# A gated recurrence with a highway layer on one core: the last product written in place, in four pieces, and a new order of all operations

## The chip, the core and the metric

The kernel runs on one core of a Trainium2 chip. Five engines work side by side, each through its own queue of instructions in order: TensorE (PE) multiplies matrices and transposes, VectorE (DVE) and ScalarE (ACT) work on tiles elementwise, GpSimd (POOL) does so more slowly and not out of PSUM, and SyncE (SP) here only issues the DMAs between the memory of the device (HBM) and the on-chip memory (SBUF). TensorE writes to PSUM. The metric is the time of one execution in device microseconds, the median of several runs.

## The reference

25344 tokens (4 sequences of 6336) of 256 channels. A recurrence along each sequence, and a highway layer on its result:

```python
    sig = 1.0 / (1.0 + np.exp(-f_logit))
    f = lower_bound[None, None, :] + (1.0 - lower_bound[None, None, :]) * sig
    i = 1.0 - f
    ...
    for t in range(S):
        h = f[:, t] * h + i[:, t] * x[:, t]
        y[:, t] = h
    ...
    H = np.maximum(x @ w_h, 0.0)
    T = 1.0 / (1.0 + np.exp(-(x @ w_t + b_t)))
    return (T * H + (1.0 - T) * x).astype(np.float32)
```

In the last three lines x stands for y of the recurrence. The result is x + T * (max(x w_h, 0) - x), and max(x w_h, 0) - x is max(x w_h - x, -x).

## The kernel before

The tokens are cut into 28 units in order: two of 256 tokens, one of 512, 23 of 1024, one of 512 and one of 256. A unit holds nb = 2, 4 or 8 blocks of 128 tokens. Per unit, with a letter for each operation (the number behind it is the unit, the one behind the point the half of the channels h or m, the block group or the piece):

- l and x load f_logit and x (SP's queue), up to 1 MB each; u = sigmoid(-l) on ScalarE.
- b (L277 to L283) is bv = u * x, in pieces of two blocks (128x512 per piece), on GpSimd, or on VectorE where the token ends in v.
- i and p transpose u and bv on TensorE into PSUM, so that channels lie on partitions and tokens along the free axis. f = 1 - (1 - lower_bound) u on ScalarE (VectorE with v).
- s (L321) is the recurrence itself, a scan along the tokens on VectorE out of f and the transposed bv. It needs the carry of the unit before, so all the s of one half stand in one chain.
- g and z (`ffn`, L329) are the two matrix products on y; t (L348) is the sigmoid of z on ScalarE; d (L352) is max(y * ncc, g) on VectorE, out of y and the PSUM of g. The factor 1 - lower_bound that the recurrence leaves out is folded into the weights and into ncc.
- E and e (L357 to L365) are e = d * t. The list `units` holds a cut for each unit: up to it, E computes in pieces of 512 on GpSimd; from it to the end (2 * tokens), one e does the rest on VectorE. There are 59 E and 16 e.
- o (L370) adds diag * y and e on TensorE, which also transposes back, in groups of four blocks; c copies it out of PSUM on ScalarE (one on VectorE); w writes it out over SP's queue.

Every tile has a tag made of its name and a slot number, `name:slot` in the list; a tile with a tag that was used before takes over that buffer once all that read the old one has run. Before, u, bv, y (4), d, t and e have three slots, f and the outputs o four, l and x six. In PSUM there are two slots of one bank (uT, bT) and three of two banks (z, g, op).

The order is written by hand as one long list of tokens, `order`: each engine gets its instructions in the order of the list (`pin` is `tc.keep_in_program_order`), and nothing reorders them. Waits between engines follow from the data and the slots. One wait is added by hand, `shared` (L203 to L209): the last VectorE instruction that is marked as sharing is held, and the next GpSimd product in the list waits for its end:

```python
        if not gpsimd:
            held[:] = [ins]
        elif held:
            tc.add_manual_dep(ins.ins, held.pop().ins.name, mybir.DependencyInfo(
                mybir.DependencyClass.Sync, mybir.DependencyReason.DATA), reason="shared port")
```

There is no such wait of VectorE for GpSimd.

Of the kernel before, what the change touches and what calls it, by code (L numbers as in the profile page):

```python
# [19 lines left out]
def kernel(  # L20
# [10 lines left out]
    nc = tc.nc  # L31
# [10 lines left out]
    units = [  # L42
        (0, 128, 2, 0, 'y', 4, 512),
        (0, 128, 2, 256, 'y', 4, 512),
        (0, 128, 4, 512, 'y', 4, 1024),
        (0, 128, 8, 1024, 'y', 4, 512),
        (0, 128, 8, 2048, 'y', 4, 512),
        (0, 128, 8, 3072, 'y', 4, 1792),
        (0, 128, 8, 4096, 'y', 4, 2048),
        (0, 128, 8, 5120, 'y', 4, 0),  # L50
        (0, 128, 8, 6144, 'y', 4, 0),
        (0, 128, 8, 7168, 'y', 4, 2048),
        (0, 128, 8, 8192, 'y', 4, 0),
        (0, 128, 8, 9216, 'y', 4, 1280),
        (0, 128, 8, 10240, 'y', 4, 2048),
        (0, 128, 8, 11264, 'y', 4, 2048),
        (0, 128, 8, 12288, 'y', 4, 2048),
        (0, 128, 8, 13312, 'y', 4, 512),
        (0, 128, 8, 14336, 'y', 4, 512),
        (0, 128, 8, 15360, 'y', 4, 512),  # L60
        (0, 128, 8, 16384, 'y', 4, 512),
        (0, 128, 8, 17408, 'y', 4, 2048),
        (0, 128, 8, 18432, 'y', 4, 256),
        (0, 128, 8, 19456, 'y', 4, 2048),
        (0, 128, 8, 20480, 'y', 4, 2048),
        (0, 128, 8, 21504, 'y', 4, 2048),
        (0, 128, 8, 22528, 'y', 4, 1024),
        (0, 128, 8, 23552, 'y', 4, 0),
        (0, 128, 4, 24576, 'y', 4, 768),
        (0, 128, 2, 25088, 'y', 4, 256),  # L70
    ]
# [21 lines left out]
b13.2 c9.1:2 i15.1:1 p12.0:0 g11.1:0 e10:2 f15.1:1 i13.0:1 w9.1 z11.1:2 t11.0:2 s12.0 o9.0:1 p13.0:0 b14.2:2 f13.0:2
t11.1 l16:4 i14.1:1 o10.1:2 b14.3 c9.0:3 f14.1:0 E11.0:0 z12.1:1 p13.1:1 b14.0 x16:4 c10.1:1 d11.1 b14.1 s13.0:0
o10.0:0 e11 w9.0 g12.0:2 t12.1:0 i15.0:0 b15.0:0 b15.1 c10.0:0 z12.0:1 s13.1 p14.1:1 f15.0:2 z13.0:0 t12.0 i14.0:0
E11.2 g12.1:1 E11.1 d12.0:0 l17:5 b15.3 g13.0:2 u16:2 s14.1:2 d12.1 t13.0:1 p14.0:1 f14.0:3 o11.1:0 o11.0:1 E12.0:1
c11.1:2 i16.0:0 b16.1:1 d13.0:1 g13.1:2 b16.3 w10.1 E12.1 w10.0 s14.0 z13.1:0 b15.2 E12.2 c11.0:3 x17:5 p15.0:1 b16.2
b16.0 E12.3 f16.0:0 l18:0 p15.1:0 d13.1 w11.0 u17:0 z14.0:1 w11.1 o12.0:2 l20:1 s15.0:3 t13.1 i16.1:1 c12.0:1 E13.3:2
w12.0 f16.1:3 s15.1 g14.0:0 x18:0 E13.0 o12.1:2 E13.1 d14.0:2 p16.1:0 t14.0:2 E13.2 z14.1:1 b17.3:2 c12.1:0 g14.1:0
u18:1 p16.0:1 s16.1:1 t14.1 z15.1:2 i17.0:0 d14.1 t15.1:0 b17.0 o13.1:0 f17.0:2 g15.0:1 b17.2 l19:2 g15.1:2 c13.1:3  # L100
s16.0 w12.1 w13.1 d15.0:0 b17.1 i17.1:1 x19:1 u20:2 o13.0:0 z15.0:1 p17.0:0 E14.2:0 f17.1v:1 d15.1 E14.0 c13.0:2
i18.0:1 z16.1:2 t15.0 g16.0:0 b18.0:0 f18.0:3 t16.1:1 E14.3 E14.1 s17.0:0 i20.0:1 l21:3 b18.1 p17.1:0 d16.0:1 b18.2
# [5 lines left out]
p20.1:0 e17 w15.1 x22:4 s20.0:1 o17.1:0 l23:5 z19.0:2 w16.1 t19.1:1 w16.0 l24:0 s20.1 i21.0:1 c17.1:3 b21.2 t19.0
g19.1:1 g19.0:0 b21.1 E18.0:1 i22.0:0 b21.3 e18 x23:5 o17.0:2 d19.1:1 l25:1 f21.0:0 f22.0:3 b22.3:1 c17.0:2 p21.0:1
u23:2 b22.1 p21.1:0 d19.0 x24:0 z20.0:1 w17.0 s21.0:0 o18.0:0 b22.2 b22.0 o18.1:2 i23.0:1 c18.0:1 g20.1:0 t20.0:2  # L110
s21.1 d20.1:2 g20.0:1 E19.2:2 p22.1:0 c18.1:0 w18.0 z21.1:2 u24:1 E19.0 E19.1 f23.0:0 w17.1 d20.0 z20.1:0 i24.1:1
E19.3 b23.3:2 s22.1:2 g21.1:1 t21.1:0 f24.1:1 t20.1 u25:0 b23.1 g21.0:2 i23.1:1 w18.1 p22.0:0 d21.1:0 l26:2 o19.0:0
d21.0 z21.0:2 s22.0 b23.0 f23.1:2 b23.2 E21.2:0 o19.1:1 t21.0 b24.3:0 p23.1:1 i25.0:0 z22.0:2 c19.1:2 x25:1 c19.0:1
l27:3 e20:1 g22.1:1 t22.0:1 w19.1 E21.0 b24.0 b24.1 s23.1:3 E20.0 b24.2 o20.1:0 p23.0:1 z22.1:2 f25.0:3 d22.1:1
i24.0:0 g22.0:1 E21.3 c20.1:3 s23.0 o20.0:0 t22.1 f24.0:2 E21.1 b25.1:1 c20.0:0 b25.2 p24.0:1 z23.0:2 d22.0 z23.1:1
w19.0 b25.0 s24.0:1 b25.3 g23.0:0 t23.0:2 w20.1 E22.1:2 t23.1 p24.1:0 u26:2 d23.0:2 o21.0:2 i25.1:1 g23.1:1 u27:1
x26:2 f25.1:0 E22.3 E22.0 x27:3 s24.1 o21.1:0 p25.0:1 c21.0:2 w20.0 i27.0:0 E22.2 d23.1 w21.0 f27.0:2 g24.0:2 i26.0:0
# [316 lines left out]
```

## Time and profile before

| | |
|---|---|
| runs, us | 212.19, 211.85, 211.55 (median 211.85) |
| span of the profiled execution, first to last instruction | 210.1 us |
| what lies around the span (median less span) | 1.75 us |
| granted TensorE clock, mean | 0.996 |
| moved by DMA | 78.69 MB, 374 GB/s over the span |

The profile gives the span of the profiled execution and no other time of it. Groups of the profile by line (busy is the time in which at least one of the group ran; instructions of one engine overlap a little at their ends):

| line, engine, result | count | busy us | mean ns |
|---|---|---|---|
| L282 POOL bv of 512 | 96 | 110.2 | 1178 |
| L359 POOL e of 512 | 54 | 61.8 | 1167 |
| L359 POOL e of 256 | 5 | 3.4 | 670 |
| L359 DVE e of 256, 768, 1024 | 3, 1, 1 | 0.8, 0.6, 0.7 | 280, 630, 684 |
| L359 DVE e of 1536, 1792, 2048 | 6, 1, 4 | 5.7, 1.1, 4.8 | 954, 1068, 1215 |
| L325 DVE scan of 1024 | 40 | 93.4 | 2340 |
| L354 DVE d of 1024 | 46 | 57.4 | 1263 |
| L282 DVE bv of 512 | 3 | 2.1 | 721 |
| L299 ACT f of 1024 | 45 | 52.8 | 1181 |
| L350 ACT t of 1024 | 46 | 53.1 | 1177 |
| L388 ACT o of 1024 | 48 | 51.1 | 1077 |

The DMA engines are at their full share up to about 175 us, and at half of it or less from 180 to 200 us. A digit of the page's slices is the busy share of a fortieth of the span, in tenths; a row of the timeline is the start and the duration in us, the engine, the line, the operation, its result and operands with shapes, the number of instructions merged into the row, and in brackets the idle time before it with what ended it.

### The profile page before, as it was taken

Reading aid. Unit: us, or ns where it says so; the run is one execution under the profiler, and the core shown is the slowest. Engines: PE = TensorE matmul, PEld = TensorE weight load, DVE = VectorE, ACT = ScalarE, POOL = GpSimd, SP = SyncE. Lnnn points to the kernel's source line nnn. Section 1 sums busy time; section 2 is a strip of 40 time slices with the busy share of each in tenths; the row PEclk is TensorE's granted clock in tenths of the full one; section 3 lists DMA queues with packets and bytes.
Section 4 is the critical chain, followed back from the end, with each engine's and each line's share of the span. In section 5 each row is a group of like instructions: output and inputs, shape, how many; then the busy total and the mean of one; then the engine's idle time right before and its main releaser. Section 6 shows DMA issues by size and latency. Waiting matters only on the chain.

```text
span 210.1 us, 4667 instructions
## 1 busy us (share of the span) xinstructions
PE 192.2 (91%) x1819; PEld 132.4 (63%) x1819; DVE 193.0 (92%) x154; ACT 194.5 (93%) x190; POOL 174.0 (83%) x166
## 2 busy tenths in 40 slices
PE   7967798899989989999999999999999899999981
PEld 2444555576655766767576667657775676776760
DVE  0689999999999999999999999999999999999950
ACT  4678999999999999999999999999999999997882
POOL 3068989789999599978999999889879969999630
PEclk9999999999999999999999999999999999999998
DMA  6999999999999999999999999999999998463486
GB/s 223 392 426 421 410 418 424 420 415 420 410 428 413 420 420 403 331 406 387 387 427 416 409 416 423 418 417 396 333 428 416 416 413 332 188 271 132 172 328 254
DMA packets 15982, 78.69 MB, mean 374 GB/s; under 512 B 1748, under 2 KB 2264, under 8 KB 10072
## 3 DMA queue, kind: packets, MB, share of 16 engines
q1 hardware_dynamic: 15952, 78.39, 92.9%
q8 instruction: 14, 0.23, 0.5%
q14 instruction: 8, 0.07, 0.1%
q10 hardware_dynamic: 8, 0.00, 0.0%
HBM read 52.43 MB, written 25.95 MB: 373 GB/s over the span
## 4 chain that ended last, share of the span: by engine, by line
DVE 34%; PE 34%; DMA 12%; issue 8%; POOL 5%; ACT 3%; SPq 1%; POOLq 0%; DVEq 0%; ACTq 0%
DVE y L325 21%; DMA x<-in_x_dram 12%; DVE d L354 10%; PE op L379 5%; PE op L378 5%; PE g L337 4%; PE z L337 4%; PE bT L308 4%; POOL bv L282 4%; PE g L140 4%; PE uT L288 4%; PE z L140 3%; DVE e L359 3%; ACT t L350 2%; ACT o L388 1%
## 5 line engine op out<-in xcount | busy, mean ns | idle before, releaser
L282 POOL TENSOR_TENSOR bv<-u,x 128x512 bf16<-128x512 f16 x96 | 110.2, 1178 | 22.3 <-DVE w_sb L235 8.9
L325 DVE TENSOR_TENSOR_SCAN y<-f,y,bT 128x1024 bf16<-128x1024 f16 (+5 forms) x54 | 107.2, 1994 | 1.4 <-issue 0.4
L359 POOL TENSOR_TENSOR e<-d,t 128x512 bf16<-128x512 bf16 (+1 forms) x59 | 65.0, 1125 | 8.3 <-DVE e L359 5.0
L354 DVE SCALAR_TENSOR_TENSOR d<-y,ncc,g 128x1024 bf16<-128x1024 bf16 (+2 forms) x56 | 63.1, 1140 | 1.8 <-PE g L337 1.3
L350 ACT ACTIVATE t<-z,bt 128x1024 bf16<-128x1024 f32 (+2 forms) x56 | 58.4, 1066 | 2.7 <-PE z L140 1.5
L299 ACT ACTIVATE f<-uT,ncc 128x1024 f16<-128x1024 f16 (+2 forms) x54 | 57.8, 1079 | 2.0 <-ACT f L299 1.0
L388 ACT COPY o<-op 128x1024 f32<-128x1024 f32 (+1 forms) x50 | 52.3, 1058 | 1.9 <-PE op L379 1.0
L274 ACT ACTIVATE u<-l 128x2048 f16<-128x2048 f32 (+2 forms) x28 | 49.0, 1760 | 4.1 <-DMA l<-in_f_logit_dram 4.1
L378 PE MATMUL op<-diag,y 128*128 128x128 f16 x396 | 49.4, 219 | 0.8 <-ACT t L350 0.5
L379 PE MATMUL op<-ident_b,e 128*128 128x128 bf16 x396 | 49.4, 219 | 0.6 <-POOL e L359 0.6
L379 PEld LDWEIGHTS <-e 128*128 128x128 bf16 x396 | 44.0, 113 | 4.6 <-POOL e L359 1.1
L378 PEld LDWEIGHTS <-y 128*128 128x128 bf16 x396 | 44.2, 113 | 2.5
L337 PE MATMUL z<-y,w_sb 128*128 128x512 bf16 (+1 forms) x112 | 39.2, 367 | 2.0 <-DVE d L354 1.0
L337 PE MATMUL g<-y,w_sb 128*128 128x512 bf16 (+1 forms) x112 | 39.6, 367 | 0.5 <-DVE y L325 0.3
L308 PE MATMUL bT<-ident_f,bv 128*128 128x128 f32 x198 | 31.9, 278 | 4.1 <-DVE y L325 1.9
L288 PE MATMUL uT<-ident_h,u 128*128 128x128 f16 x396 | 31.1, 220 | 4.5 <-DVE y L325 3.3
L288 PEld LDWEIGHTS <-u 128*128 128x128 f16 x396 | 26.3, 98 | 13.9 <-issue 7.4
L140 PE MATMUL g<-y,w_sb 128*128 128x512 bf16 x92 | 34.9, 379 | 0.0
L140 PE MATMUL z<-y,w_sb 128*128 128x512 bf16 x92 | 34.8, 379 | 0.0
L337 PEld LDWEIGHTS <-w_sb 128*128 128x128 f16 x224 | 21.6, 98 | 16.2 <-issue 0.8
L308 PEld LDWEIGHTS bT<-ident_f,bv 128*128 128x128 f32 x198 | 22.3, 141 | 12.0 <-POOL bv L282 4.5
L140 PEld LDWEIGHTS <-w_sb 128*128 128x128 f16 x184 | 17.9, 98 | 18.2 <-issue 3.9
(35 smaller groups left out, 47.1 us busy)
## 6 DMA issues: line engine op xcount, KB each, us to landing
out_dram<-o SPq DMA_DIRECT2D x48, 512.0 KB, 6.1
l<-in_f_logit_dram SPq DMA_DIRECT2D x23, 1024.0 KB, 10.2
x<-in_x_dram SPq DMA_DIRECT2D x23, 1024.0 KB, 11.1
l<-in_f_logit_dram SPq DMA_DIRECT2D x2, 512.0 KB, 9.2
x<-in_x_dram SPq DMA_DIRECT2D x2, 512.0 KB, 6.0
l<-in_f_logit_dram SPq DMA_DIRECT2D x3, 256.0 KB, 6.1
x<-in_x_dram SPq DMA_DIRECT2D x3, 256.0 KB, 5.4
out_dram<-o SPq DMA_DIRECT2D x3, 256.0 KB, 5.4
```

The costliest lines, as they stand in the source:

```text
L140: return pe.add_instruction(mybir.InstMatmult(name=nc.get_next_instruction_name(), start_tensor_calc=start, stop_tensor_calc=stop, tile_si ...
L282: shared(pin(e.tensor_mul(st[n]["bv"][:, k].rearrange("p d j -> p j d"), st[n]["u"][:, q:q + 2], st[n]["x"][:, q:q + 2])), not eng)
L288: pin(nc.tensor.transpose(uT[:, j * P:(j + 1) * P], st[n]["u"][:, j, h * P:(h + 1) * P], ident_h))
L299: pin(nc.scalar.activation(to, of, AF.Identity, scale=ncc[:, h:h + 1], bias=1.0))
L308: pin(nc.tensor.transpose(words[:, k:k + g * (P - 1) + 1:g], pair, ident_f))
L325: pin(nc.vector.tensor_tensor_scan(y[:, c:e], st[n]["f", h][:, c:e], st[n]["bT", h][:, c:e], 0.0 if fresh else carry[h], op0=ALU.mult, op1 ...
L337: pin(nc.tensor.matmul(p[:, a:e], w, half(n, "y", ki)[:, a:e], start=ki == 0, stop=ki == NH - 1))
L350: pin(nc.scalar.activation(half(n, "t", m), st[n]["z", m][:, :tokens(n)], AF.Sigmoid, bias=bt[:, m:m + 1]))
L354: pin(nc.vector.scalar_tensor_tensor(half(n, "d", m), half(n, "y", m), ncc[:, m:m + 1], st[n]["g", m][:, :tokens(n)], op0=ALU.mult, op1=AL ...
L359: shared(pin(eng.tensor_mul(st[n]["e"][:, a:e], st[n]["d"][:, a:e], st[n]["t"][:, a:e])), eng is nc.gpsimd)
L378: pin(nc.tensor.matmul(o, half(n, "y", h)[:, cols], diag[:, h], start=True, stop=False))
L379: pin(nc.tensor.matmul(o, half(n, "e", h)[:, cols], ident_b, start=False, stop=True))
```

## The change

The cut per unit is gone. `do_e` computes one of two (256-token units: 256 wide; 512: 512 wide) or four pieces of 512 and writes it over d; the token says by a v at its end that VectorE does it, and else GpSimd. There is no tile e any more, and o reads d:

```diff
-    def times(n, eng, a, e, slot):
-        flat(n, "e", "e", slot)
-        shared(pin(eng.tensor_mul(st[n]["e"][:, a:e], st[n]["d"][:, a:e], st[n]["t"][:, a:e])), eng is nc.gpsimd)
-
-    def do_E(n, k, eng, slot):
-        times(n, nc.gpsimd, k * 512, min(units[n][6], k * 512 + 512), slot)
-
     def do_e(n, k, eng, slot):
-        times(n, nc.vector, units[n][6], NH * tokens(n), slot)
+        a, c = units[n][3][k:k + 2]
+        e = nc.vector if eng else nc.gpsimd
+        shared(pin(e.tensor_mul(st[n]["d"][:, a:c], st[n]["d"][:, a:c], st[n]["t"][:, a:c])), not eng)
...
-                pin(nc.tensor.matmul(o, half(n, "e", h)[:, cols], ident_b, start=False, stop=True))
+                pin(nc.tensor.matmul(o, half(n, "d", h)[:, cols], ident_b, start=False, stop=True))
```

The units are the same, written by a formula; b is written with the same pieces of two blocks:

```diff
+    parts = [2] * 2 + [4] + [8] * 23 + [4] + [2]
+    units, at = [], 0
+    for nb in parts:
+        units.append((nb, at, {2: (0, 1), 4: (0, 1, 2), 8: (0, 1, 2, 3, 4)}[nb], {2: (0, 256, 512), 4: (0, 512, 1024), 8: (0, 512, 1024, 1536, 2048)}[nb]))
+        at += nb * P
```

The list is a new one from the first token to the last. Its beginning and end before and after:

```diff
-pc:1 l0:0 u0:0 l3:1 wh cc dg i0.0:1 x0:0 i0.1:0 k*16 u3:1 wt WH b0.0v:0 l1:2 f0.0:0 f0.1:1 p0.1:0 i3.1:1 u1:2 s0.1:0
+l1:0 x0:0 x1:1 wt l0:1 u1:0 wh l2:2 l3:3 b1.0v:0 x2:2 x3:3 l4:0 pc:0 x4:4 i1.0:0 l7:4 cc i1.1:1 u0:0 b0.0:1 l5:5 dg
+f1.1:0 k*16 f1.0v:1 u2:1 i0.1:0 WH i0.0:1 f0.0:2 f0.1v:3 p0.0:0 WT p0.1:1 s0.0:0 s0.1 b2.0:1 i2.0:0 f2.0v:2 u3:0 b2.1
+g0.1:0 p1.0:1 z0.1:1 z0.0:2 s1.0:1 t0.1:0 p1.1:0 s1.1 i3.0:1 d0.1:0 t0.0 f3.0:0 i2.1:0 g1.0:1 b3.1:0 x5:1 f2.1v:1 b3.2
+z1.1:0 g1.1:2 t1.1:1 p2.1:0 i3.1:1 g0.0:0 b3.0 f3.1:3 d1.1:1 e1.1 z1.0:2 e0.1 b3.3v u4:1 d0.0 s2.1:2 p2.0:1 s2.0
...
-E26.1 w24.1 d27.0 z27.0:2 c25.1:1 w25.0 t27.0 E26.0 o26.0:1 w25.1 c26.0:3 e27:0 E27.0 o27.0:2 c27.0:0 w26.0 w27.0
+s27.0:0 w23.1 c24.0:1 s27.1 g26.0:1 t26.0 d26.0:0 g26.1:0 e25.2 c25.1:3 d26.1 w24.1 w23.0 e26.0v w24.0 z27.0:2 t27.1:0
+w25.1 o25.0:1 g27.0:0 e26.1v c25.0:0 o26.0:2 d27.0:1 z27.1:0 t27.1 g27.1:1 c26.0:1 w25.0 w26.0 d27.1 e27.1v e27.0v
+o27.0:0 c27.0:2 w27.0
```

What the two lists hold, counted:

| | before | after |
|---|---|---|
| bv on GpSimd, on VectorE | 96, 3 | 97, 2 |
| e on GpSimd: of 512, of 256 | 54, 5 | 61, 3 |
| e on VectorE | 16, of 256 to 2048 | 35 of 512, 3 of 256 |
| f on VectorE | one of 1024, one of 256 | two of 512, two of 256 |
| o copied by VectorE | one of 512 | one of 1024 |
| slots named: u, bv, d | 3, 3, 3 | 4, 3, 4 |
| slots named: l, x | 6, 6 | 6, 5 |

More of the change, by code (lines that the diff above doesn't have):

```diff
@@ L39 @@
     firsts = [b * S for b in range(B)]
[L42 to L71, printed above, removed]
@@ L93 @@
[L93 to L97, printed above, removed]
@@ L98 @@
[L98 to L102, printed above, removed]
@@ L108 @@
[L108 to L112, printed above, removed]
@@ L113 @@
[L113 to L117, printed above, removed]
@@ L118 @@
-c21.1:1 o22.1:1 s25.0:0 f26.0:1 E23.2:1 b26.0:2 z24.0:0 p25.1:0 d24.0:0 c22.1:3 b26.1 t24.0:0 E23.0 i26.1:1 z24.1:1
-f26.1:3 o22.0:0 g24.1:2 E23.1 w21.1 i27.1:1 s25.1 w22.1 t24.1 g25.0:1 c22.0:0 z25.0:0 b27.0:0 d24.1 d25.0:1 p26.0:0
-f27.1:0 E23.3 o23.0:2 p26.1:1 E24.0:0 z25.1:1 t25.0:1 g25.1:0 s26.0:2 c23.0:2 s26.1 z26.0:2 t25.1 d25.1 p27.1:1
-t26.0:2 o23.1:1 g26.1:2 e24 s27.1:3 o24.0:0 d26.1:2 c23.1:1 w22.0 z26.1:1 E24.1 c24.0:3 p27.0:1 w23.0 w23.1 t26.1
-e25:2 s27.0 w24.0 o24.1:2 c24.1:0 g26.0:0 o25.0:1 g27.1:2 c25.0:2 d26.0 o25.1:0 e26:1 d27.1:0 g27.0:2 z27.1:1 t27.1:0
@@ L123 @@
[L123 removed]
+    parts = [2] * 2 + [4] + [8] * 23 + [4] + [2]
[3 more added lines that the diff above has]
+        at += nb * P
+    assert at == B * S
+    order = """
+l1:0 x0:0 x1:1 wt l0:1 u1:0 wh l2:2 l3:3 b1.0v:0 x2:2 x3:3 l4:0 pc:0 x4:4 i1.0:0 l7:4 cc i1.1:1 u0:0 b0.0:1 l5:5 dg
@@ new lines @@
+e10.3 t11.0:0 b15.2:0 b15.0 x14:0 t11.1 o9.0:2 l18:2 b15.3 i14.1:0 e11.0 b15.1 b14.2:2 e11.1v b14.0 o9.1:0 f14.1:0
+p13.0:1 b14.1 e11.3v e11.2v s13.0:1 z12.1:1 c9.1:0 c9.0:2 i15.1:0 e10.1v g12.1:0 f15.1:2 z12.0:2 p13.1:1 d12.1:2 x17:1
+i15.0:0 s13.1 t12.1:0 o10.1:0 t12.0 f15.0:3 g12.0:1 b14.3 e12.2 g13.0:2 e12.3 i14.0:0 w9.1 c10.1:1 g13.1:0 u18:0 d12.0
+d13.0:3 l16:0 o10.0:1 p14.1:1 d13.1 f14.0:1 c10.0:3 s14.1:2 z13.0:2 b17.1:1 z13.1:0 p14.0:0 w9.0 s14.0 o11.0:1 t13.0:1
+t13.1 e12.1 p15.1:1 o11.1:0 u16:1 s15.1:0 z14.0:2 b17.3 p15.0:0 e12.0 c11.1:0 b17.0 x16:2 b16.2:0 c11.0:2 l20:1 w10.0
@@ new lines @@
+z14.1:0 i16.0:1 b16.1 b16.0 t14.0:0 g14.0:1 s15.0 g14.1:2 t14.1 o12.0:0 i16.1:0 w10.1 d14.0:0 w11.1 b16.3 e14.1
+o12.1:1 f16.0:0 p16.0:1 u20:3 e13.3 e13.1 d14.1 b17.2 w11.0 f16.1:1 x18:0 c12.0:1 e14.0 g15.1:2 b18.3:2 c12.1:0 e13.0v
+e13.2v s16.0:3 b18.0 d15.1:1 i17.1:0 z15.0:0 l19:0 b18.1 b18.2 z15.1:1 e14.3v f17.1:2 p16.1:1 i18.1:0 e14.2v t15.0:1
+s16.1 o13.0:2 g15.0:0 t15.1 o13.1:1 w12.0 f18.1:0 d15.0 p17.1:0 c13.0:2 c13.1:3 u19:1 e15.3 e15.0 e15.2 w12.1 z16.1:2
+i17.0:1 x19:2 f17.0:1 g16.0:0 o14.0:1 c14.0:0 b19.3:0 l21:1 s17.1:1 d16.0:2 p17.0:0 w13.0 b19.0 i19.1:1 t16.1:0 b19.1
@@ new lines @@
+i21.1:1 w15.0 t19.1:1 f21.1:0 e18.0 o17.1:2 p20.0:0 l24:1 s20.0 o17.0:0 c17.1:0 i21.0:1 e19.3 e18.3 c17.0:2 g19.0:1
+f21.0:1 w16.0 e18.1 z19.0:2 u24:0 p21.1:0 x22:2 d19.0 o18.0:0 z20.0:1 p21.0:1 b22.0:1 b22.3 c18.0:1 s21.1:1 b22.1
+s21.0 w16.1 b22.2 g20.1:0 d20.1:0 l23:2 t19.0 i22.1:0 g20.0:2 d20.0 w17.1 e19.1 w17.0 t20.0:0 e19.0 z20.1:1 i22.0:1
+f22.1:0 u23:2 x23:0 b23.3:0 b23.2 b23.0 f22.0:1 g21.0:0 t20.1 p22.0:0 o18.1:2 c18.1:0 e19.2v d21.0:3 w18.0 p22.1:1
+s22.0:2 z21.0:0 t21.0:1 e21.0 l25:0 b23.1 x24:1 b24.0:1 e20.3v o19.0:1 e20.2 e20.1v s22.1 o19.1:2 b24.2 c19.0:1 w18.1
@@ new lines @@
+d24.0:2 z24.1:2 c22.0:2 t24.1 e22.3 i26.0:1 o22.1:0 g24.1:1 s25.1 c22.1:3 z25.0:2 g25.1:0 f26.0:1 t25.0:2 b26.1:0
+b26.0 i26.1:0 e23.1v e23.3 d24.1 o23.1:1 l27:1 z25.1:2 e24.1v e23.0v d25.1:1 u27:1 f26.1:0 p26.1:0 w21.0 e23.2 e24.3v
+e24.0 p26.0:1 c23.1:1 o24.1:0 t25.1 e24.2 o23.0:1 s26.0:2 b27.0:0 w21.1 i27.0:1 s26.1 w22.0 e25.3 c24.1:0 c23.0:2
+f27.0:0 g25.0:2 z26.1:0 i27.1:0 w22.1 d25.0 e25.1v o24.0:1 e25.0v t26.1:0 p27.1:1 f27.1:1 z26.0:0 p27.0:0 o25.1:2
+s27.0:0 w23.1 c24.0:1 s27.1 g26.0:1 t26.0 d26.0:0 g26.1:0 e25.2 c25.1:3 d26.1 w24.1 w23.0 e26.0v w24.0 z27.0:2 t27.0:1
@@ L191, in tokens @@
     def tokens(n):
-        return units[n][1] * units[n][2]
+        return units[n][0] * P
     def pieces(n):
-        at, N = units[n][3], tokens(n)
+        at, N = units[n][1], tokens(n)
         cuts = [0] + [c - at for c in firsts if at < c < at + N] + [N]
@@ L255, in rows @@
     def rows(full, n, j0, j1):
-        at = units[n][3]
+        at = units[n][1]
         return full[at + j0 * P:at + j1 * P, :].rearrange("(p j) d -> p j d", p=P)
     def load(n, name, src, slot):
-        nb = units[n][2]
+        nb = units[n][0]
         t = sb([P, NB, D], FP32, name, slot)
@@ L271, in do_u @@
     def do_u(n, k, eng, slot):
-        nb = units[n][2]
+        nb = units[n][0]
         u = sb([P, NB, D], FP16, "u", slot)
@@ L279, in do_b @@
             st[n]["bv"] = sb([P, NB // 2, D, 2], BF16, "bv", slot)
-        q = 2 * k
+        a, c = units[n][2][k:k + 2]
         e = nc.vector if eng else nc.gpsimd
-        shared(pin(e.tensor_mul(st[n]["bv"][:, k].rearrange("p d j -> p j d"), st[n]["u"][:, q:q + 2],
-                                st[n]["x"][:, q:q + 2])), not eng)
+        shared(pin(e.tensor_mul(st[n]["bv"][:, a:c].rearrange("p k d j -> p k j d"),
+                                st[n]["u"][:, 2 * a:2 * c].rearrange("p (k j) d -> p k j d", j=2),
+                                st[n]["x"][:, 2 * a:2 * c].rearrange("p (k j) d -> p k j d", j=2))), not eng)
     def do_i(n, h, eng, slot):
         uT = one_bank(slot, FP16, "uT")
-        for j in range(units[n][2]):
+        for j in range(units[n][0]):
             pin(nc.tensor.transpose(uT[:, j * P:(j + 1) * P], st[n]["u"][:, j, h * P:(h + 1) * P], ident_h))
@@ L291, in do_f @@
     def do_f(n, h, eng, slot):
-        N, nb = tokens(n), units[n][2]
+        N, nb = tokens(n), units[n][0]
         f = sb([P, NB * P], FP16, "f", slot)
@@ L304, in do_p @@
         words = bT.bitcast(FP32)
-        g = units[n][2] // 2
+        g = units[n][0] // 2
         for k in range(g):
```

53 lines of the change are left out of this document (28 added, 25 removed).

## The prediction

> **What bounds the kernel now.** I read the busy shares and slices of the page first, then its groups by line, then the waits, then the timelines of GpSimd and VectorE side by side.
>
> ```profile
> PE 192.2 (91%) x1819; PEld 132.4 (63%) x1819; DVE 193.0 (92%) x154; ACT 194.5 (93%) x190; POOL 174.0 (83%) x166
> ...
> DVE  0689999999999999999999999999999999999950
> ACT  4678999999999999999999999999999999997882
> POOL 3068989789999599978999999889879969999630
> ...
> L359 POOL TENSOR_TENSOR e<-d,t 128x512 bf16<-128x512 bf16 (+1 forms) x59 | 65.0, 1125 | 8.3 <-DVE e L359 5.0
> ```
>
> VectorE and ScalarE are full from the fifth slice almost to the end; each runs its own queue without a hole, and the span is their 193 to 195 us plus a start and a tail. Only GpSimd (POOL) has holes. The waits say what most of them are:
>
> ```profile
> POOL bv L282 <- DVE w_sb L235: 8.9, 1, 8.9
> POOL bv L282 <- DVE e L359: 7.8, 6, 2.4
> ...
> POOL e L359 <- DVE e L359: 5.0, 4, 2.8
> ```
>
> The columns are the waiter, what ended the wait, the total in us, how often, the longest. Apart from the start, the holes are GpSimd standing still while VectorE does its share of e: `shared` makes a GpSimd product wait for the last VectorE product listed before it. What the two do at one moment is seen in the timelines, GpSimd first:
>
> ```profile
> 43.09 1.16 POOL L359 TENSOR_TENSOR e<-d,t 128x512 bf16<-128x512 bf16 x1
> 45.29 5.67 POOL L282 TENSOR_TENSOR bv<-u,x 128x512 bf16<-128x512 f16 x5 [1.05 <-PE bT L308]
> ...
> 73.36 6.83 POOL L282 TENSOR_TENSOR bv<-u,x 128x512 bf16<-128x512 f16 x6 [2.41 <-DVE e L359]
> 80.13 2.28 POOL L359 TENSOR_TENSOR e<-d,t 128x512 bf16<-128x512 bf16 x2
> ...
> 112.10 5.67 POOL L359 TENSOR_TENSOR e<-d,t 128x512 bf16<-128x512 bf16 x5
> 117.68 4.59 POOL L282 TENSOR_TENSOR bv<-u,x 128x512 bf16<-128x512 f16 x4
> ```
> ```profile
> 39.75 0.94 DVE L359 TENSOR_TENSOR e<-d,t 128x1536 bf16<-128x1536 bf16 x1
> ...
> 44.05 1.01 DVE L359 TENSOR_TENSOR e<-d,t 128x1536 bf16<-128x1536 bf16 x1
> ```
>
> Nowhere in this trace does a VectorE product lie over a GpSimd product by more than 0.2 us: the list places each one where GpSimd has just finished. The one that began 0.20 us before a GpSimd product ended (44.05, against 43.09 + 1.16 = 44.25) took 1.01 us; its like at 39.75, with GpSimd idle, 0.94. So the little overlap there is was mostly paid back in length. I read the two engines as taking turns, and count their products in one **ledger**.
>
> By the Trainium skill, SBUF — State Buffer, section "SBUF: two separate sides", a VectorE operation with two SBUF inputs and a GpSimd operation that reads SBUF exclude each other for a whole instruction. By that rule the ledger is exact and the span is what follows below; by the row alone, which shows 0.07 us for 0.20, it may be looser, as in the first rival. The trace agrees as far as 0.20 us goes.
>
> **The change part by part.** *GpSimd's own work.* From starts to next starts a bv product takes (80.13 - 73.36)/6 = 1.13 us, a 512-wide e (117.68 - 112.10)/5 = 1.12, a 256-wide e 0.63 (its rows). Before, GpSimd has 96 bv, 54 e of 512 and 5 of 256; after, 97, 61 and 3. That is +1.1 + 7.8 - 1.3 = **+7.6 us**.
>
> *VectorE's share of e.* The trace has no 512-wide e on VectorE. From 1024 (0.684) and 2048 (1.215) a line gives 0.418; it cannot be under the 256 row (0.280) or over the 768 row (0.630). In VectorE's own queue consecutive instructions overlap, so starts count: 0.19 for 256 (51.97 to 52.16), 0.56 for 768 (97.16 to 97.72), so about 0.34 for 512. After: 35 x 0.34 + 3 x 0.19 = 12.5 us. Before, 16 larger ones: 3 x 0.19 + 0.56 + 0.61 + 6 x 0.87 + 0.99 + 4 x 1.13 = 12.5. Equal, although VectorE does fewer elements. Two f of 256 and two of 512 instead of one of 256 and one of 1024: +0.5; one o copy of 1024 (bounded by 0.61, the 512 row, and twice that; I take 1.15) for one of 512: +0.5; one bv less: -0.6. VectorE's sum: **+0.4 us**. ScalarE loses about 1.6 us by the same moves (one o of 1024 at 1.06 becomes one of 512 at 0.6; its f sum falls by about 1). TensorE's matmuls are the same; the second operand of o is now d.
>
> *In place, and the buffers.* A product that writes its own input reads and writes as much as before; no row shows it in place, and I take the 1.12 us of the same product into e; the nearest other row, bv with its stride at 1.13, bounds it at 0.01 either way, 0.6 us over 61. The list names u 0 to 3 and d 0 to 3, but bv only 0 to 2, and x now 0 to 4 (before 0 to 5): the fourth bv is not used. d now stays until o has read it, which is what the fourth d pays for. The loads move on SP's queue past each other and past the writes; DMA is full until 175 us in both, 78.39 MB, and 52.43 MB of reads at some 300 GB/s over 175 us leave the loads units ahead, so I cost that at nothing; if the cover is gone, one wait for x is 0.4 to 1.0 us (the two rows at 28.92 and 33.91).
>
> *The ledger.* GpSimd's second bv (b2.0) starts at 12.53 us, released by x2. The same nine loads, 3.5 MB, stand up to x2 in both lists, so b2.0 cannot start sooner after; b0.0 merely moves forward into idle time. From 12.53 to the end of the last GpSimd product (205.24) before: 95 x 1.13 + 54 x 1.12 + 5 x 0.63 = 171.1 of 192.7 us; 21.6 idle, 14.6 of it behind VectorE. After: 96 x 1.13 + 61 x 1.12 + 3 x 0.63 = 178.7, and before the last GpSimd product (e25.2) VectorE has 33 e of 0.418, one of 0.28 and one bv of 0.67: 14.7. The turns change some 25 times; where GpSimd waits, each costs 0.11 more than the VectorE product (idle 1.28 for 0.94, 2.41 for 2.36, 1.42 for 1.20, on average), where VectorE waits, nothing; I take half, 1.4. So e25.2 ends at 12.5 + 178.7 + 14.7 + 1.4 = **207.3 us**, with no wait for data at all (before, 7 us of them).
>
> *The tail.* Behind e25.2 in TensorE's queue: o25.0 (16 matmuls, 203.21 to 204.04 before: 0.9), g27.0 0.4, o26.0 0.9, z27.1 and g27.1 0.8; then d27.1 on VectorE 0.5, its e27.1 and e27.0 0.5, and from the end of the last product to the end 210.1 - 205.24 = 4.9. Sum 8.9. **Span 207.3 + 8.9 = 216.2 us**, against 210.1. The median of the runs shown (211.85) lies 1.75 above the span; 216.2 + 1.75 = **218.0 us**.
>
> *A second route.* The ledger up to the last bv of unit 25, then VectorE from its first scan on. Before: 166.7 us of products, 12.5 of start and 1.4 of turns give 180.6; bT 0.5; VectorE has 17.1 left: 198.2, and it really ended at 203.5: 5 us of slack. After: 93 x 1.13 + 51 x 1.12 + 3 x 0.63 + 27 x 0.418 + 0.28 + 0.67 = 176.4, so 190.2; then 18.1: 208.8. The ledger has moved from 5 us under the real end to 5 us over it. With 4.9 behind VectorE's last product the span is at least 213.7 that way. Stretch by stretch, the ledger grows against VectorE's sum from unit 14 on: s14.0 to s22.1, +67 us against +57.
>
> **The rivals.** *The turns are not exclusive* (the other side): a VectorE e running over a GpSimd product costs neither anything. Then GpSimd needs 178.7 from 12.5 on and has room, and VectorE sets the end again: s3.1 can start at 19.1 (x3 is there by 15.1; bv 0.6, two d 0.8, two scans 2.4, e 0.2) in place of 19.60, the sum is +0.4, and the last e sits on VectorE, so 4.9 us follow its end at 203.5 and not 6.6. Span 203.5 - 0.5 + 0.4 + 4.9 = 208.3, time **210.1**. It decides as soon as the e of VectorE cost GpSimd under 6 of the 14.7 us. For it: the list keeps GpSimd's own work level with VectorE's all along (5.7 us less at s3.1, 7.3 less at s26.1). Against: the 1.01 us row, and 14.6 us of waits now.
>
> *Half exclusive*: half the 14.7 us is saved; ledger 200, VectorE's queue with some stalls decides: **213**.
>
> *VectorE pays, too*: where VectorE comes to an e while GpSimd is in a product, it waits half of one, 0.56 us, in some 24 groups: 13.4 us in the queue that has no holes. 203.5 + 0.4 + 13.4 + 4.9 = 222.2, time **224**. Against: if GpSimd is the later one, VectorE has that time to spare.
>
> **How the numbers follow.** Forecast 0.64 (its own range 215 to 221.5: no turn cost and a shorter tail below, 3 to 5 us of waits for data above), half exclusive 0.10, both pay 0.10, not exclusive 0.16. About 0.3%, 0.64 us, is what a measurement of this kernel can tell from no change. Faster than 211.2: most of the 0.16, 0.13. Within: 0.05 from the two nearest cases. Slower: 0.82. The range 211 to 222.5 leaves out about half of the first rival and most of the case at 224.
>
> **What would show it.** Right: GpSimd busy 181 to 183 us, its waits behind VectorE's e small in total or VectorE idle for bT and behind bv from unit 14 on, ScalarE and VectorE no longer full, GpSimd and VectorE's e hardly overlapping. Wrong: VectorE full to the end with its e lying over GpSimd products at 0.42 us each; or bv waits for x in the middle; or GpSimd's product in place at another duration than 1.12 to 1.17.

## The result and the profile after

The changed kernel takes 231.79 us (median of four runs, 228.14 to 234.12) against 211.74 (211.55 to 212.19) for the kernel before. Executions over 1.5% above the fastest of their kernel count as slow, here two of the four with the profiled one (232.61) among them; the ratio, 1.084 with a 95% interval of 1.077 to 1.091, and all ratios below leave them out, while medians are of all runs. It is slower, as forecast, but by 18 us by the ratio and 20 by the medians, and not by 6. The profiled execution has a span of 230.8 us. From its page, the busy times and two rows of the slices:

```profile
PE 197.3 (85%) x1792; PEld 137.2 (59%) x1819; DVE 213.7 (93%) x177; ACT 195.6 (85%) x188; POOL 186.6 (81%) x172
...
DVE  0879999999899999999969999999999999999881
ACT  3475899986899779999558998799899998989983
```

VectorE is full almost to the end; ScalarE, full before, now has holes. VectorE's busy time went from 193.0 to 213.7 us: 20.7 more, just what the span grew by (210.1 to 230.8). So I take VectorE to have set the end before and after, and the question is which of its instructions got longer. The groups by line of the same page, then the one of VectorE's e in the kernel before:

```profile
L260 POOL TENSOR_TENSOR bv<-u,x 128x512 bf16<-128x512 f16 x97 | 114.4, 1208 | 19.7 <-ACT u L252 7.8
L339 POOL TENSOR_TENSOR d<-d,t 128x512 bf16<-128x512 bf16 (+1 forms) x64 | 73.1, 1159 | 14.9 <-DVE d L333 4.9
...
L339 DVE TENSOR_TENSOR d<-d,t 128x512 bf16<-128x512 bf16 (+1 forms) x38 | 32.7, 891 | 0.1
```
```profile
L359 DVE TENSOR_TENSOR e<-d,t 128x1536 bf16<-128x1536 bf16 (+5 forms) x16 | 13.7, 863 | 0.4 <-ACT t L350 0.3
```

VectorE's share of e takes 32.7 us, mean 891 ns; before it was 13.7 for more elements. That is 19.0 of the 20.7. Single instructions from the timeline of VectorE show two kinds of e of the same 512 columns, beside GpSimd's products in the timeline of GpSimd at the same time (start, duration, both in us):

```profile
28.55 0.42 DVE L339 TENSOR_TENSOR d<-d,t 128x512 bf16<-128x512 bf16 x1
...
43.52 3.98 DVE L339 TENSOR_TENSOR d<-d,t 128x512 bf16<-128x512 bf16 x3
...
50.87 1.30 DVE L339 TENSOR_TENSOR d<-d,t 128x512 bf16<-128x512 bf16 x1
```
```profile
29.14 1.15 POOL L339 TENSOR_TENSOR d<-d,t 128x512 bf16<-128x512 bf16 x1 [1.29 <-DVE d L339]
...
40.04 11.85 POOL L260 TENSOR_TENSOR bv<-u,x 128x512 bf16<-128x512 f16 x10
```

At 28.55 GpSimd stands and waits, and e takes 0.42 us. At 43.52 and 50.87 GpSimd is in the middle of ten bv without a pause, and each e takes 1.30 to 1.40. Taken one by one, an e that begins while a GpSimd product runs ends about 0.28 us after that product's end. Of the 35 e of 512, 21 met a product that way (in 10 groups between 43 and 187 us); they last 27.1 us in all, and at 0.42 each they would last 8.8: **18.3 us**, 0.87 per meeting. Eight more began in about the last 0.2 us of a product and paid next to nothing (0.39 to 0.49 us each).

Why did the hand-made wait not keep them apart? The ten bv at 40.04 are, in GpSimd's order, b6.0, b6.3, b6.2, b6.1, b8.3, b7.2, b7.0, b7.3, b7.1 and b8.2. In the list e4.2v stands just ahead of b8.2, so the wait sits on b8.2. But when VectorE came to e4.2v, at 43.52, GpSimd had just begun the fourth of the ten, b6.1 (43.42 to 44.59); b8.2 was six products away, and nothing held b6.1 or VectorE. The waits of GpSimd for VectorE's e say the same (waiter, what ended it, us in total, times, longest):

```profile
POOL d L339 <- DVE d L339: 4.4, 6, 1.3
...
POOL bv L260 <- DVE d L339: 1.3, 1, 1.3
```

Before, GpSimd's e stood 5.0 us that way and its bv 7.8, in 10 waits; now, with more than twice as many e on VectorE, it is 4.4 and 1.3, in 7. The waits did not get dear, as the forecast had it: for most e they do not happen.

### The profile page after: what moved, and what is told of

It reads as the page before. It is cut to its first block, busy times and chain, and to the rows that moved or that the text cites. A ratio compares the mean times of both kernels' runs of the same rounds, so it can differ in the third digit from the quotient of the medians.

```text
span 230.8 us, 4668 instructions
## 1 busy us (share of the span) xinstructions
PE 197.3 (85%) x1792; PEld 137.2 (59%) x1819; DVE 213.7 (93%) x177; ACT 195.6 (85%) x188; POOL 186.6 (81%) x172
## 4 chain that ended last, share of the span: by engine, by line
DVE 41%; PE 35%; issue 13%; ACT 6%; DMA 2%; SPq 0%; DVEq 0%; ACTq 0%
DVE y L304 22%; DVE d L339 9%; DVE d L333 8%; PE g L316 6%; PE uT L267 5%; PE op L352 5%; PE op L353 5%; PE z L316 4%; PE g L118 4%; PE bT L287 4%; PE z L118 2%; ACT f L278 2%; DMA x<-in_x_dram 2%; ACT o L362 2%; ACT u L252 1%
## 5 line engine op out<-in xcount | busy, mean ns | idle before, releaser
L260 POOL TENSOR_TENSOR bv<-u,x 128x512 bf16<-128x512 f16 x97 | 114.4, 1208 | 19.7 <-ACT u L252 7.8
L339 POOL TENSOR_TENSOR d<-d,t 128x512 bf16<-128x512 bf16 (+1 forms) x64 | 73.1, 1159 | 14.9 <-DVE d L333 4.9
L278 ACT ACTIVATE f<-uT,ncc 128x1024 f16<-128x1024 f16 (+2 forms) x52 | 55.3, 1067 | 11.9 <-PE uT L267 11.8
L329 ACT ACTIVATE t<-z,bt 128x1024 bf16<-128x1024 f32 (+2 forms) x56 | 56.0, 1030 | 4.5 <-DVE d L339 1.5
L362 ACT COPY o<-op 128x1024 f32<-128x1024 f32 (+1 forms) x50 | 49.5, 1002 | 7.9 <-PE op L353 7.2
L353 PE MATMUL op<-ident_b,d 128*128 128x128 bf16 x396 | 51.2, 223 | 2.4 <-DVE d L339 2.4
L352 PE MATMUL op<-diag,y 128*128 128x128 f16 x396 | 51.4, 223 | 2.2 <-DVE d L333 1.4
L353 PEld LDWEIGHTS <-d 128*128 128x128 bf16 x396 | 44.8, 115 | 7.4 <-DVE d L339 3.3
L267 PEld LDWEIGHTS <-u 128*128 128x128 f16 x396 | 27.9, 103 | 13.8 <-issue 7.7
L339 DVE TENSOR_TENSOR d<-d,t 128x512 bf16<-128x512 bf16 (+1 forms) x38 | 32.7, 891 | 0.1
L118 PE MATMUL z<-y,w_sb 128*128 128x512 bf16 x85 | 32.2, 379 | 0.0
```

What stands on the lines that cost most here:

```text
L118: return pe.add_instruction(mybir.InstMatmult(name=nc.get_next_instruction_name(), start_tensor_calc=start, stop_tensor_calc=stop, tile_si ...
L260: shared(pin(e.tensor_mul(st[n]["bv"][:, a:c].rearrange("p k d j -> p k j d"), st[n]["u"][:, 2 * a:2 * c].rearrange("p (k j) d -> p k j d" ...
L267: pin(nc.tensor.transpose(uT[:, j * P:(j + 1) * P], st[n]["u"][:, j, h * P:(h + 1) * P], ident_h))
L278: pin(nc.scalar.activation(to, of, AF.Identity, scale=ncc[:, h:h + 1], bias=1.0))
L329: pin(nc.scalar.activation(half(n, "t", m), st[n]["z", m][:, :tokens(n)], AF.Sigmoid, bias=bt[:, m:m + 1]))
L339: shared(pin(e.tensor_mul(st[n]["d"][:, a:c], st[n]["d"][:, a:c], st[n]["t"][:, a:c])), not eng)
```

## The experiments

The theories, as the expectations name them: A, VectorE stands until GpSimd's running product ends, and meets one because GpSimd trails the list, so the one-sided wait sits too late; B, the ledger of the prediction, in which the two take turns and GpSimd pays; C, a product in place is dear; D, VectorE's price goes by the columns. Each kernel was run beside the kernel before on its chip (211.59 to 211.78 us there).

### The price of a meeting by itself

A kernel that computes nothing of the reference: streams of products of VectorE and GpSimd, alone and together, each stage closed by an 8-column product on either engine that reads the other's.

```diff
+    def v512(out, n=512):
+        pin(nc.vector.tensor_mul(out[:, :n], va[:, :n], vb[:, :n]))
+
+    def g512(k):
+        pin(nc.gpsimd.tensor_mul((pc if k % 2 else pd)[:, 512:1024], pa[:, :512], pb[:, :512]))
...
+    # 3: both, V in products of 512
+    for k in range(20):
+        g512(k)
+    for k in range(10):
+        v512(vc)
+    meet()
```

> No part of the reference is computed: short streams of VectorE and GpSimd products of bf16, alone and together, 512 wide unless said. Theory A (VectorE stands until the GpSimd product that runs has ended, GpSimd hardly notices): alone 0.42 and 1.15 us; together, VectorE 1.3 to 1.4 us each in a row and GpSimd 1.3 to 1.35; VectorE products of 2048 about 2.1 us each; in place the same as out of place; with one operand in PSUM no lengthening (0.65 to 0.7 us). Theory B (the ledger of the prediction, each in turn, one costs the other its whole length): GpSimd 1.15 + 0.42 = 1.57 each beside VectorE's. Theory C (in place itself is dear): the in-place stage is longer than the same out of place by 0.4 us or more.

Timeline of VectorE: eight products alone (11.58), ten of 512 beside GpSimd's stream (25.75), five of 2048 (49.87), ten in place (98.12, where the stream had ended), ten with one operand in PSUM beside the stream (104.07); L64 is the 8-column product.

```profile
11.58 3.64 DVE L67 TENSOR_TENSOR vc<-va,vb 128x512 bf16<-128x512 bf16 x8
...
25.75 13.05 DVE L67 TENSOR_TENSOR vc<-va,vb 128x512 bf16<-128x512 bf16 x10
...
49.87 10.60 DVE L67 TENSOR_TENSOR vc<-va,vb 128x2048 bf16<-128x2048 bf16 x5
...
76.07 22.13 DVE L64 TENSOR_TENSOR vd<-back,vb 128x8 bf16<-128x8 bf16 x1 [14.57 <-POOL back L63]
98.12 4.55 DVE L97 TENSOR_TENSOR vd<-vd,vb 128x512 bf16<-128x512 bf16 x10
...
104.07 7.17 DVE L103 TENSOR_TENSOR vc<-va,pm 128x512 bf16<-128x512 bf16 x10
...
125.36 26.55 DVE L64 TENSOR_TENSOR vd<-back,vb 128x8 bf16<-128x8 bf16 x1 [13.46 <-POOL back L63]
```

And GpSimd's products in the same stretches, one without VectorE, one beside the products of 512, one beside those of 2048:

```profile
24.66 1.15 POOL L70 TENSOR_TENSOR pd<-pa,pb 128x512 bf16<-128x512 bf16 x1
...
29.46 1.33 POOL L70 TENSOR_TENSOR pd<-pa,pb 128x512 bf16<-128x512 bf16 x1
...
50.99 2.13 POOL L70 TENSOR_TENSOR pd<-pa,pb 128x512 bf16<-128x512 bf16 x1
```

A product of 512 on VectorE takes 0.42 us alone and 1.25 beside the stream; one of 2048 takes 2.05, against 1.22 for such an e in the kernel before (1215 ns). Both pay 0.83: the price goes by the meeting and not by the column, and D falls. GpSimd pays little for a narrow product (1.33 instead of 1.15, not the 1.57 of B) and more for a wide one (2.13). With an operand in PSUM no price shows: 0.69 us each and GpSimd's at 1.15 throughout, though such a product of 512 was not measured alone. In place costs the same as out of place, 0.42, though it was measured without GpSimd, since the stage before it began only when the stream was over. That was the unforeseen part: at 76.07 an 8-column product (0.16 us alone) stood for the whole stream, 20 GpSimd products, 22.13 us, and at 125.36 for 24 of them, 26.55 us. So a meeting can cost VectorE one product, or all that follow without a pause.

### In place alone

The kernel before with its list and cuts, e written over d, d in four slots.

```diff
-        flat(n, "d", "d", slot)
+        flat(n, "d", "d", n % 4)
...
-        shared(pin(eng.tensor_mul(st[n]["e"][:, a:e], st[n]["d"][:, a:e], st[n]["t"][:, a:e])), eng is nc.gpsimd)
+        shared(pin(eng.tensor_mul(st[n]["d"][:, a:e], st[n]["d"][:, a:e], st[n]["t"][:, a:e])), eng is nc.gpsimd)
```

> The kernel before, its order and its cuts, with e written over d, d in four slots, and o reading d. Theory A: in place and the fourth buffer cost nothing, 211 to 212.5 us. Theory C: 16 e of VectorE and 59 of GpSimd in place are longer; by the 0.5 us per e that the changed kernel shows more than its 0.42, 8 us on VectorE, 219 to 221 us.

211.25 us (211.07 to 211.38) against 211.59, ratio 0.9982, interval 0.9973 to 0.9992; VectorE's e 13.7 us as before. C falls. This part of the change is by itself no loss, and a gain of at most 0.3%.

### The wait taken out of the kernel before

```diff
-        if not gpsimd:
-            held[:] = [ins]
-        elif held:
-            tc.add_manual_dep(...)
+        return
```

> The kernel before without the hand-made waits of GpSimd for VectorE's products. Theory A: the 13 longer e of VectorE and two bv meet a GpSimd product in the middle and pay half of one on average, 0.56 us, 7 to 9 us in VectorE's full queue: 216 to 221 us, and the e rows of VectorE grow by about 0.5 us each. Theory B (taking turns, only the sum counts): GpSimd's 14.6 us of waits fall away and nothing else happens, 210 to 212 us.

222.7 us (221.22 to 225.15), ratio 1.0471, interval 1.0449 to 1.0493. The same list, the same 16 e on VectorE, and only the wait gone: VectorE's e go from 13.7 to 23.6 us and the time up by 10 to 11. B expected no loss, and falls; A's range, 216 to 221, is passed by a little. The group of VectorE's e:

```profile
L355 DVE TENSOR_TENSOR e<-d,t 128x1536 bf16<-128x1536 bf16 (+5 forms) x16 | 23.6, 1478 | 0.4 <-ACT t L346 0.3
```

A single e of 1536 columns took seven microseconds; the timelines of VectorE and of GpSimd there:

```profile
134.08 7.07 DVE L355 TENSOR_TENSOR e<-d,t 128x1536 bf16<-128x1536 bf16 x1
```
```profile
133.59 1.17 POOL L355 TENSOR_TENSOR e<-d,t 128x512 bf16<-128x512 bf16 x1
134.70 4.53 POOL L278 TENSOR_TENSOR bv<-u,x 128x512 bf16<-128x512 f16 x4
139.18 1.16 POOL L355 TENSOR_TENSOR e<-d,t 128x512 bf16<-128x512 bf16 x1
140.34 4.08 POOL L278 TENSOR_TENSOR bv<-u,x 128x512 bf16<-128x512 f16 x3
```

VectorE came 0.49 us into a GpSimd product, was passed over by five more, and got in during the next. So the lock-out of the streams happens in the kernel too.

### Less work on GpSimd

The changed kernel with each of GpSimd's pieces of e cut to its first 256 columns; the rest of those pieces is left out.

```diff
+        if not eng:
+            c = min(c, a + 256)
```

> The changed kernel, with each of GpSimd's e pieces only on its first 256 columns (the rest of these pieces of e is left out, so that d stands there). All pieces, waits and orders stay. GpSimd saves 61 x 0.49 = 30 us and keeps up with the list. Theory A: the hand-made waits now hold it back in front of VectorE's e, whose mean falls from 0.94 to 0.45 to 0.6 us; VectorE's busy time from 214 to 195 to 200 us; 211 to 218 us. If the number of pieces, the place or the order of the other work is what costs (theory C and others): e stays near 0.9 us and the time at 226 us or more.

224.11 us (222.17 to 226.67), ratio 1.0559, interval 1.0509 to 1.0608. A miss: theory A expected at most 218. VectorE's e fell only from 32.7 to 26.6 us, and GpSimd's busy time from 186.6 to 156.7. Of the 35 e of 512 on VectorE 17 still met a product (21 in the changed kernel), the last at 177 us. The price of a meeting came out as A has it: an e that met one of the halved products took 0.88 us instead of 1.38 (at 102.81, 127.28 and 177.06), since the product in its way ended sooner. So the theory of the meeting is kept, and the reading that GpSimd's load alone makes it late falls. That it trails since its second bv starts only at 13.8 us and many bv stand in a row is likely, but was not tried.

### Fewer, wider products on VectorE

Neighbouring pieces of one unit that VectorE computes are joined, 38 to 29 products.

```diff
+        if (n, k) in merged:
+            ks = merged[n, k]
...
+            a, c = units[n][3][ks[0]], units[n][3][ks[-1] + 1]
```

> The changed kernel with VectorE's pieces of e that follow each other in one unit made one instruction: 38 become 29, columns unchanged. Theory A (a price for each meeting with a running GpSimd product, 0.83 to 1.0 us whatever the width, as the short streams showed): 8 of the meetings fall away, VectorE's busy time falls by 7 to 9 us, 221 to 225 us. Theory D (VectorE runs at a lower rate beside GpSimd, a price by the column): VectorE's e together stay at 31 us or more and the time at 228 us or more.

228.10 us, with runs of 221.70, 228.05, 228.16 and 228.60, too far apart for an interval. The profiled one (span 226.3) suggests why: three pieces of e11 in one product of 1536 were locked out.

```profile
100.12 8.45 DVE L349 TENSOR_TENSOR d<-d,t 128x1536 bf16<-128x1536 bf16 x1
```

As they stand, the time and VectorE's e (31.7 us) are what D forecast, although the streams had ruled D out. Without those 8.45 us the time would stand near the run at 221.70, which fits A; but that is worked out, not shown.

### GpSimd's products later in the list

If the wait sits on products that GpSimd has not reached yet, the remedy is to put GpSimd's products later in the list: then those that it is really doing stand behind VectorE's e, and wait. Each is moved five products on, as far as its readers and buffers allow. Around e4:

```diff
-b7.0 c3.0:2 p6.0:1 f7.1:2 z5.1:0 t5.1:1 b7.3 b7.1 e4.2v b8.2 l9:2 e4.0v e4.1 e4.3v d5.1:1 l11:3 w3.1 e5.3 o4.0:1
+b6.1 p6.0:1 f7.1:2 z5.1:0 t5.1:1 e4.2v b8.3:1 l9:2 e4.0v b7.2:2 e4.3v d5.1:1 l11:3 w3.1 b7.0 b7.3 b7.1 b8.2 e4.1
```

> The changed kernel with the GpSimd products set five products later in the list wherever their readers and the buffers allow it; the order on each engine stays as it is, only the hand-made waits now sit on products that GpSimd has not yet begun when VectorE comes. Theory A: GpSimd stands still in place of VectorE; VectorE's e fall to a mean of 0.45 to 0.6 us, its busy time from 214 to 195 to 202 us, and the time to 213 to 222 us, GpSimd's ledger (219.6 by the prediction's sum) being the upper side. Rival: GpSimd falls back by as much again, the meetings stay, 226 us or more.

> Both edits together. Theory A: what remains of the meetings is shorter; VectorE's busy time 193 to 199 us, 212 to 220 us, and no less than after_yield5 by more than 3 us. Rival (the two save the same meetings only in part, or the lag follows): between after_merge and after_yield5, or above 222 us.

234.91 us (ratio 1.1066, interval 1.1004 to 1.1128), and with joined pieces 233.04 (1.1048, 1.098 to 1.1116). Both miss A's ranges (213 to 222 and 212 to 220): VectorE's e fell to 23.9 and 22.2 us, but the time did not. By e23.1 the first of the two stood at 202.1 us, where the changed kernel stands at 211.6; all of that was lost in the last 30 us. The waits of the first kernel between 200 and 231 us:

```profile
POOL d L339 <- DVE d L339: 9.0, 3, 4.3
PEld L353 <- POOL d L339: 7.2, 3, 2.6
PE op L353 <- POOL d L339: 6.7, 3, 2.5
...
DVE y L304 <- PE bT L287: 5.6, 2, 3.8
```

At the end of the list GpSimd is no longer late, so a product placed five later only waits for VectorE, TensorE waits for it, and the scans behind that wait for TensorE. So the next kernel moves the products only up to e20.3v and leaves the rest of the list alone; another does so by eight products:

> The changed kernel with GpSimd's products standing five products later in the list (where readers and buffers allow it) only up to e20.3v; from there on the list is the changed kernel's own. Theory A (VectorE's e meets products because GpSimd trails the list; the loss of the run with the later products over the whole list came in its last 30 us, where GpSimd's late products hold up the matmuls): the gain of the first part stays. There that run stood 9.5 us ahead of the changed kernel at e23.1 (202.1 against 211.6 us), so 231.8 - 9.5 = 222, range 218 to 226; VectorE's e sum 24 to 27 us instead of 33.8. Rival: the later products cost the matmuls as much as they save VectorE wherever they stand, and nothing is left: 230 to 236.

> The same with eight products instead of five. Theory A: GpSimd trails by four to six products, so eight reach past it nearly everywhere that readers and buffers allow; a little fewer meetings than with five (e sum 21 to 26 us) and 216 to 225 us. Rival: GpSimd's products come too late for the transposes of bv and for the matmuls that read e, and eight is worse than five: over 228 us.

By five: 223.57 us (222.43 to 224.93), ratio 1.0562, interval 1.0517 to 1.0607, against 1.084 for the changed kernel: **about 6 us less** (8.2 by the medians) with nothing but the list altered. VectorE's e of 512 by shape and GpSimd's wait for them, from the groups and from the waits:

```profile
L339 DVE TENSOR_TENSOR d<-d,t 128x512 bf16<-128x512 bf16 x35 | 23.6, 705 | 0.0
```
```profile
POOL d L339 <- DVE d L339: 9.9, 12, 1.7
```

The mean went from 943 to 705 ns, and the wait from 4.4 to 9.9 us: it bites again. Two e beside GpSimd's timeline, at the place where in the changed kernel the same two took 2.66 us:

```profile
75.83 0.77 DVE L339 TENSOR_TENSOR d<-d,t 128x512 bf16<-128x512 bf16 x2
```
```profile
74.82 1.17 POOL L260 TENSOR_TENSOR bv<-u,x 128x512 bf16<-128x512 f16 x1 [0.20 <-DMA x<-in_x_dram]
76.69 3.41 POOL L260 TENSOR_TENSOR bv<-u,x 128x512 bf16<-128x512 f16 x3 [0.69 <-DVE d L339]
```

By eight: 235.99 us (ratio 1.117, 1.1132 to 1.1208). The e fell further, to 22.3 us, but GpSimd stood 25.8 us for VectorE's e (11.7 before bv, 14.1 before e), and what it makes came late. The rival was right there: eight is too many.

### Both together

> The first of these three with VectorE's neighbouring pieces of one unit joined, but for the three of e11 (which, joined, were locked out for 8.45 us): 38 products of VectorE become 31. Theory A: each meeting costs VectorE about 0.83 us whatever its width, so seven fewer, of which half met a product: 3 us below the kernel with five products later in the first part, 215 to 223 us, e sum 20 to 24 us, unless one of them is locked out for many products. Rival (the price goes by column): no gain over that kernel.

231.40 us (1.0929, 1.0879 to 1.0979). By an oversight in its list, the token that should end the later placing had been joined away, so the products stood later to the very end; it is to be read against the 234.91 above. With the end put right:

> In the kernel before this one the token e20.3v, at which the later placing was to end, had gone into the joined piece, so its products stood later to the very end (231.4 us, beside 234.9 for the same without joined pieces: 3.5 us less). Here the later placing ends at e20.1v. Theory A (each meeting costs VectorE the same whatever the width; late products hurt only in the last 30 us): 223.6 for the unjoined one, less the 3 us: 217 to 223 us, e sum 21 to 24 us. Rival (joining gains nothing, or a wider product is locked out): 223 us or more.

220.66 us (220.43 to 221.12), ratio 1.0422, interval 1.0405 to 1.0440. Seven products fewer on VectorE, 2.9 us less than the same list with single pieces, as A expected. Its groups by line (L346 are three of the joined products):

```profile
L349 DVE TENSOR_TENSOR d<-d,t 128x512 bf16<-128x512 bf16 (+2 forms) x28 | 17.6, 650 | 0.4
L346 DVE TENSOR_TENSOR d<-d,t 128x1024 bf16<-128x1024 bf16 x3 | 3.0, 1009 | 0.0
```

Set side by side, the time follows VectorE's e almost one for one, whatever the edit, but for the kernels in which GpSimd's products come too late (the last two rows):

| kernel | VectorE's e, us | 211.7 + (e - 13.7) | measured, us |
|---|---|---|---|
| before; in place alone | 13.7; 13.7 | 211.7 | 211.7; 211.25 |
| joined, five later in the first part | 20.6 | 218.6 | 220.66 |
| before without the wait | 23.6 | 221.6 | 222.7 |
| five later in the first part | 24.3 | 222.3 | 223.57 |
| half of GpSimd's e | 26.6 | 224.6 | 224.11 |
| joined pieces | 31.7 | 229.7 | 228.1 |
| the change | 32.7 | 230.7 | 231.79 |
| later over the whole list (single, joined; joined but e11) | 23.9, 22.2; 21.7 | 221.9, 220.2; 219.7 | 234.91, 233.04; 231.40 |
| eight later in the first part | 22.3 | 220.3 | 235.99 |

(The e are those of one profiled execution, the times medians; beside the profiled executions' own times, 222.17 for half of GpSimd's e and 232.61 for the change, the middle column is off by up to 2.4 us. Which rows to leave out was decided after the runs.)

## Why the prediction was wrong, and where it was right

**The step that failed** is the price of VectorE's e: "Equal, although VectorE does fewer elements", with "VectorE's sum: +0.4 us", and in the ledger "where VectorE waits, nothing". Each e was priced at 0.34 us from start to start, as if it ran alone. That is what it takes where it meets no product (28.55 to 28.89); where it meets one it takes some 1.3 (three from 43.52 to 47.42). 21 of 35 met one, 18.3 us in the one queue that had no holes.

**The rule was right, its payer was not.** The prediction leaned on the Trainium skill, SBUF — State Buffer, section "SBUF: two separate sides": whichever of the two operations starts first holds the shared ports for its whole instruction and the other blocks. The trace agrees on the block (1.30 us at 50.87 instead of 0.42). I charged the turns to GpSimd, as the list of before has it, and let VectorE arrive at free ports. In fact GpSimd, in the middle of a run of products, came first. The row at 44.05, which the prediction read for the turns, already showed who pays: VectorE's e got longer (1.01 for 0.94), and GpSimd's product kept its 1.16. The page's rule doesn't say that the one that is blocked may be passed over by several products, as at 134.08; there the measurement decides.

**The rival that had it**, "VectorE pays, too", came to 224 with 24 groups of half a product, 13.4 us. Its mechanism is what the traces show, and it was given 0.10. Its size was low since every piece of a run meets a product of its own (three e at 43.52: 3.98 us) and pays 0.87, not 0.56. The argument against it, "if GpSimd is the later one, VectorE has that time to spare", was the error: a VectorE that is 92% busy and sets the end spares nothing, and being ahead of GpSimd in the list is the very state in which the one-sided wait does not hold.

**The ledger** put the end of e25.2 at 207.3 us; it was 221.8. GpSimd's start was 1.3 later than taken (13.79 for 12.5: the load of x2 came later than in the old order). Its products from there took 183.8 us instead of 178.7, part of it the stretching where VectorE slips in (bv 1208 ns for 1178, e of 512 1183 for 1167). It stood 5.7 us behind VectorE's e where 16.1 had been set for e and turns, and 18.5 us for other things where none had been set: mostly for d, t and bT, behind a late VectorE. 1.3 + 5.1 - 10.4 + 18.5 = 14.5, the whole miss of the span. That these 18.5 us come from VectorE is read from what ended the waits (bT 5.2 us, d 4.9, t 4.4), not from a run.

**Right:** the direction, but by another path, since VectorE's queue and not the ledger set the end; GpSimd's added products at 1.12 us from start to start (+7.6 forecast; busy +12.6 with the stretching); in place and the fourth d at nothing (measured 0.18% less); the tail behind e25.2, 8.9 forecast, 230.8 - 221.8 = 9.0 measured, by luck: up to the end of the last product it was 4.7 for 4.0, and from there 4.3 for 4.9. The sign given by "what would show it wrong" came in part: VectorE full to the end with its e lying over GpSimd's products, though not at 0.42 us each. The rivals in which the turns are not exclusive fall with the first experiment.

**Open:** take the 18.3 us out of the span and 212.5 remain, 2.4 over before. Two more VectorE products met one of GpSimd's in that trace: a conversion of w_sb at 8.48 took 1.30 us instead of 0.35 behind b0.0, and b3.3 at 17.63 took 1.53 instead of 0.72, 1.8 us together. That leaves 0.6, near the +0.4 that the forecast had for VectorE's sum. No list of the new kind without any meeting was run, and what the lower granted clock (0.953 in the mean, 0.996 before) adds was not taken apart.

## What to carry to other kernels

A wait that keeps two engines off a shared port in one direction works only while the engine that waits is level with the list; before moving work, ask for each instruction what the other engine will really be doing when it comes up, not what stands beside it in the list. Price such work by meetings and not by columns: in the streams one product of 2048 that met paid the same 0.83 us as one of 512, so one wide one is cheaper than four narrow ones, unless it is locked out (8.45 us). The cost belongs in the main to the engine that comes second, which is dear if that engine has no holes. And put a product later only where its engine is late: the same move that saved some 6 us in the first part cost more than that again at the end.

## What the hardware showed that was not expected

- VectorE can be passed over. An 8-column product stood for 20 and 24 GpSimd products (22.13 and 26.55 us), one of 1536 for 7.07 us and another for 8.45 in the kernels, while others in the same traces were let in after one product. What decides this was not found.
- The granted TensorE clock fell in some stretches of the changed kernel: 0.66 and 0.83 from 10 to 30 us, 0.83 from 50 to 60 and 0.67 from 110 to 120. Windows of the changed kernel (stretch, length, busy time and instructions of PE, PEld, DVE, ACT and POOL, granted clock, DMA share, GB/s):

```profile
10.00:20.00 10.00, 7.79 (x48) 5.63 (x48) 8.66 (x16) 7.24 (x9) 6.00 (x5) 0.66 1.01 421
...
110.00:120.00 10.00, 6.34 (x39) 4.24 (x41) 8.16 (x6) 5.93 (x5) 9.22 (x9) 0.67 1.01 401
```

  Before, the clock was 1.00 in every window up to 200 us, also from 10 to 20 us with TensorE busy for only 6.28 of the 10. So the busy time of a window does not tell its clock, and the cause stays open. TensorE's busy time rose from 192.2 to 197.3 us for the same matmuls; how much of the time hangs on that was not tried.
